# Keys and queries of three chunks as 2x2 block products, seven in place of eight, in a gated linear-attention and Mish kernel

## The chip, the cores and the metric

The kernel runs on one core of a Trainium2 chip. The metric is the device time of one execution, in microseconds (us), lower is better. Engines: PE (matrix products, with its weight load PEld), DVE (VectorE), ACT (ScalarE), POOL (GpSimd), SP (SyncE, which here only issues transfers). SBUF and PSUM are the on-chip memories; PE writes only PSUM, in banks of 128x512 fp32. A DMA moves data between DRAM and SBUF.

## The reference

x is 2048 rows of 512. Two branches read it and a gate mixes them:

```python
qkv = x @ wqkv                       # 512 -> q, k, v, 32 heads of 16
pq, pk = q @ w_phi, k @ w_phi        # per head, 16 x 16
phi = concat(softmax(p), softmax(-p))          # 32 features per head, of pq and of pk
kv = sum over rows of phi_k^T v ;  z = sum over rows of phi_k
o  = (phi_q kv) / (phi_q z + 1e-6) ; a = o @ wo
b  = mish(x @ w1 + b1) @ w2          # 512 -> 1376 -> 512
out = g * a + (1 - g) * b ,  g = sigmoid(sum(x * gate_w))
```

All is fp32. A product is made of three fp32r products: with each operand split as high + low part, high*high + high*low + low*high.

## The kernel before, in words

w_phi is first folded into the key and query weights on PE ("fuse"), so that one product of x gives pk or pq. Then come two stages.

Stage A goes over eight chunks of 256 rows (two tiles of 128, t = 0 and 1). Per chunk and tile PE makes three products, k (pk), v and q (pq), of 12 matmuls each: four slices of 128 of the 512 inputs times three of high/low. That is 72 matmuls for a chunk. After every second chunk the matmuls `kvp` add phi_k^T v of the last two chunks, 128 small ones. DVE turns each pk tile into features in nine steps, named in the order text as follows: `mx`, `mn` (maximum and minimum per head), `d0`, `d1` (p - max and min - p, into tile E of 128x1024), then after ACT's exponential (`E`) `S` (sums per head), `rS` (reciprocal), `ml` (E times the reciprocal). `z` adds E to zacc on POOL (L318): both operands 128x1024 in SBUF. ACT copies v and q out of PSUM (`ve`, `qe`); q goes to DRAM (pqd) for stage B. The next chunk's x is split by ACT (`xh`) and POOL (`xl`, L248). Two pieces of 128x1024 of w1 and w2 are split for stage B in every chunk: `wh` on ACT, `wl` on POOL (L370).

Stage B goes over four blocks of 512 rows: up projection, Mish, down projection, and the attention output of the same rows.

Order is written by hand. Texts such as EVEN, ODD, NEXT, LAST name the steps; `run` carries them out left to right, and every instruction is pinned to its place in its engine's queue. A step with `'` is of the previous chunk, one with `+` of the next. An engine runs its queue strictly in that order; between engines semaphores make an instruction wait for what it reads and for the buffer it overwrites. The E tiles have four buffers, PSUM tag "a" three banks and "dn" four, the x tiles ("tx") two.

```python
def proj(x, t, wh, wl, tag):
    for a, w in ((xh, wh), (xh, wl), (xl, wh)):
        for k in range(KT):
            mm(ps, a[k // 2][:, k % 2, sl], w[:, k, :], ...)
at(key, f"z{t}", lambda d=d: pin(G_.tensor_add(zacc, zacc, d["E"])))
run((EVEN, ODD)[c % 2] if c < NCH - 2 else NEXT if c < NCH - 1 else LAST, ("A", c), ("A", c - 1), ("B", 0))
```

All matmuls are recorded under the helper `mm` (L101), all ACT operations under `act` (L121), so the profile is read by tile names.

Of the kernel before, what the change touches and what calls it, by code (L numbers as in the profile page):

```python
# [15 lines left out]
P = 128  # L16
# [17 lines left out]
WARM = 6  # L34

# [16 lines left out]
    lq0+ k0 xh mx0 mn0 d00 d10 xl ldx k1 wh0 E0 wl0 ldw0 mx1 mn1 d01 d11 wh1 E1 S0 rS0 ml0 z0 v0 ve0 wl1 ldw1
# [37 lines left out]
def tile_gated_mix(ctx: ExitStack, tc: tile.TileContext, xT, wv, wkT, wqT, bd, w1a, w1b, b1, w2a, w2b, wo, out):  # L90
# [159 lines left out]
    def feat_ops(key, t, src, d):  # L250
# [7 lines left out]
        def dd(a):  # L258
# [3 lines left out]
            if a == 0:  # L262
# [16 lines left out]
    def scale_by(d, eng):  # L279
        pin(eng.tensor_mul(hv(d["E"][:, :]), hv(d["E"][:, :]), d["S"][:, :, None].to_broadcast([P, 2 * H, DH])))  # L280

    def a_ops(c):
        key = ("A", c)
        P_ = psA[c] = {}
        for t in range(2):
# [19 lines left out]

            def st(t=t):
# [11 lines left out]
            at(key, f"z{t}", lambda d=d: pin(G_.tensor_add(zacc, zacc, d["E"])))  # L318
# [14 lines left out]
        at(key, "kv", kv)  # L333
        if c + 1 < NCH:
# [6 lines left out]
            for j in range(2):  # L341
                at(key, "xl", lambda j=j: x_lo(c + 1, j, G_))
# [431 lines left out]
```

## Time and profile before

| | |
|---|---|
| runs | 456.2, 456.25 and 458.14 us, median 456.25 |
| span of the profiled execution, first to last instruction | 455.6 us; 0.65 us less than the median run |
| mean granted TensorE clock | 0.998 |
| PE busy | 445.6 us, 98% of the span |
| DVE, ACT, POOL busy | 306.8, 195.0 and 161.4 us |
| chunk 0's products start / chunk 1's / chunk 2's | 10.67 / 30.28 / 48.62 us |
| first matmuls of stage B's first block | 153.34 us |

A row of the timeline reads: start, duration (us), engine, line, operation, output <- inputs, shapes, how often, and in brackets the idle time before it with what ended it. An instruction's duration includes its start-up and its end, which overlap the neighbours', so instructions that follow each other closely start closer together than they last. A group by line gives the total and the mean in ns.

### The profile page before, as it was taken

Reading aid. Unit: us, or ns where it says so; the run is one execution under the profiler, and the core shown is the slowest. Engines: PE = TensorE matmul, PEld = TensorE weight load, DVE = VectorE, ACT = ScalarE, POOL = GpSimd, SP = SyncE. Lnnn points to the kernel's source line nnn. Section 1 sums busy time; section 2 is a strip of 40 time slices with the busy share of each in tenths; the row PEclk is TensorE's granted clock in tenths of the full one; section 3 lists DMA queues with packets and bytes.
Section 4 is the critical chain, followed back from the end, with each engine's and each line's share of the span. In section 5 each row is a group of like instructions: output and inputs, shape, how many; then the busy total and the mean of one; then the engine's idle time right before and its main releaser. Section 6 shows DMA issues by size and latency. Waiting matters only on the chain.

```text
span 455.6 us, 6980 instructions
## 1 busy us (share of the span) xinstructions
PE 445.6 (98%) x2772; PEld 363.4 (80%) x2772; DVE 306.8 (67%) x402; ACT 195.0 (43%) x265; POOL 161.4 (35%) x102
## 2 busy tenths in 40 slices
PE   7999999999999899999899999999999999999996
PEld 6888888888888678878687887887887888787885
DVE  2599459369399999799987985666967629611002
ACT  3554443443334645726337354434254553234220
POOL 3338777767862355221123212023212122221211
PEclk9999999999999999999999999999999999999999
DMA  7721513505523110313434050332041402030002
GB/s 284 247 83 56 168 53 129 186 8 179 183 82 106 47 23 2 94 46 86 146 94 138 17 158 14 108 115 54 23 119 53 112 19 94 1 81 13 1 1 92
DMA packets 25593, 40.07 MB, mean 88 GB/s; under 512 B 5716, under 2 KB 13908, under 8 KB 25560
## 3 DMA queue, kind: packets, MB, share of 16 engines
q1 hardware_dynamic: 25384, 39.35, 28.4%
q8 instruction: 22, 0.36, 0.3%
q10 hardware_dynamic: 144, 0.26, 0.2%
q14 instruction: 11, 0.09, 0.1%
q0 software_dynamic: 32, 0.01, 0.0%
HBM read 22.82 MB, written 8.40 MB: 69 GB/s over the span
## 4 chain that ended last, share of the span: by engine, by line
PE 61%; DVE 4%; ACT 1%; issue 0%
PE up L101 25%; PE down L101 24%; PE wo L101 10%; PE num L101 2%; DVE xbl L403 1%; DVE Sm L269 1%; DVE T L548 0%; DVE Dn L552 0%; DVE io L633 0%; ACT L121 0%; DVE tt L566 0%; DVE E L280 0%; DVE Dn L572 0%; ACT E L121 0%; DVE Sm L277 0%; ACT io L121 0%
## 5 line engine op out<-in xcount | busy, mean ns | idle before, releaser
L498 POOL TENSOR_TENSOR l<-act,h 128x512 fp32r<-128x512 f32 x44 | 60.7, 1380 | 224.2 <-ACT h L121 189.4
L121 ACT ACTIVATE act<-up,b1s 128x512 f32<-128x512 f32 x44 | 30.3, 689 | 91.5 <-PE up L101 90.3
L318 POOL TENSOR_TENSOR zacc<-zacc,E 128x1024 f32<-128x1024 f32 x16 | 39.7, 2482 | 45.8 <-DVE E L280 31.4
L121 ACT ACTIVATE E<-E 128x1024 f32<-128x1024 f32 x32 | 33.6, 1059 | 49.4 <-DVE E L265 49.4
L280 DVE TENSOR_TENSOR E<-E,Sm 128x1024 f32<-128x1024 f32 x32 | 44.0, 1375 | 1.1
L101 PE MATMUL wo<-woh,ohl 128*128 128x512 f32 x128 | 40.8, 390 | 1.2 <-DVE ohl L607 1.2
L269 DVE TENSOR_REDUCE Sm<-E 128x64 f32<-128x1024 f32 x32 | 38.7, 1209 | 3.8 <-ACT E L121 3.8
L101 PE MATMUL down<-w2ah,h 128*128 128x512 f32 x96 | 37.5, 390 | 0.0
L101 PE MATMUL down<-w2al,h 128*128 128x512 f32 x96 | 37.4, 389 | 0.0
L101 PE MATMUL down<-w2ah,l 128*128 128x512 f32 x96 | 37.4, 389 | 0.0
L633 DVE SCALAR_TENSOR_TENSOR io<-down,og_sb,io 128x512 f32<-128x512 f32 x16 | 11.3, 751 | 31.1 <-PE down L101 31.0
L256 DVE TENSOR_REDUCE mx<-proj 128x32 f32<-128x512 f32 x16 | 11.0, 689 | 30.8 <-PE proj L101 30.8
L101 PE MATMUL down<-w2bh,h 128*128 128x512 f32 x80 | 31.2, 391 | 0.0
L101 PE MATMUL down<-w2bl,h 128*128 128x512 f32 x80 | 31.1, 389 | 0.0
L101 PE MATMUL down<-w2bh,l 128*128 128x512 f32 x80 | 31.1, 389 | 0.0
L101 PEld LDWEIGHTS wo<-woh,ohl 128*128 128x128 f32 x128 | 24.0, 188 | 6.6 <-DVE ohl L607 1.6
L121 ACT ACT_TABLE_LOAD x19 | 24.4, 1283 | 10.1 <-PE up L101 9.8
L121 ACT ACTIVATE h<-act 128x512 fp32r<-128x512 f32 x44 | 27.8, 632 | 1.4
L607 DVE TENSOR_TENSOR ohl<-num,ohl 128x512 fp32r<-128x512 f32 x16 | 10.2, 678 | 26.4 <-ACT ohl L121 26.4
L101 PE MATMUL up<-xbl,w1ah 128*128 128x512 f32 x96 | 25.8, 391 | 1.5 <-DVE xbl L403 1.5
L101 PE MATMUL up<-xbh,w1ah 128*128 128x512 f32 x96 | 26.3, 396 | 0.2 <-ACT zb L121 0.2
L101 PE MATMUL up<-xbh,w1al 128*128 128x512 f32 x96 | 25.7, 389 | 0.0
(113 smaller groups left out, 970.6 us busy)
## 6 DMA issues: line engine op xcount, KB each, us to landing
xraw<-in_xT_dram SPq DMA_DIRECT2D x16, 512.0 KB, 4.8
eT<-tt SPq DMA_DIRECT2D x128, 64.0 KB, 2.0
pqd<-qs SPq DMA_DIRECT2D x16, 256.0 KB, 3.5
pq<-pqd SPq DMA_DIRECT2D x16, 256.0 KB, 2.8
out_dram<-io SPq DMA_DIRECT2D x16, 256.0 KB, 2.1
raw<-in_w1a_dram SPq DMA_DIRECT2D x3, 512.0 KB, 3.6
raw<-in_w2a_dram SPq DMA_DIRECT2D x3, 512.0 KB, 3.7
wT<-in_wkT_dram SPq DMA_DIRECT2D x4, 256.0 KB, 5.4
```

Of the source, the lines that this page charges most:

```text
L101: return pin(nc.tensor.matmul(*a, **k))
L121: return pin(A_.activation(out_, in_, fn, **k))
L256: pin(V.tensor_reduce(d[name], hv(src()), axis=AX.X, op=op))
L269: pin(V.tensor_reduce(d["S"], hv(d["E"][:, :]), axis=AX.X, op=ALU.add))
L280: pin(eng.tensor_mul(hv(d["E"][:, :]), hv(d["E"][:, :]), d["S"][:, :, None].to_broadcast([P, 2 * H, DH])))
L318: at(key, f"z{t}", lambda d=d: pin(G_.tensor_add(zacc, zacc, d["E"])))
L403: pin(V.tensor_sub(xb[b][1][:, :, sl], kt(raw[h], SC), f32(xb[b][0][:, :, sl])))
L498: pin(G_.tensor_sub(U[i]["l"], U[i]["a"], f32(U[i]["h"])))
L607: pin(V.tensor_sub(ohl[h, gp][:, 512:], num[h, gp], f32(ohl[h, gp][:, :512])))
L633: pin(V.scalar_tensor_tensor(io[t], dn[t], og_sb[:, i : i + 1], io[t], op0=ALU.mult, op1=ALU.add))
```

## The change

**Products.** In chunks 2, 3 and 4 (FAST) keys and queries are one product: x of the chunk as 2x2 blocks (row tile by half of the inputs) times the weights as 2x2 blocks (half of the inputs by key/query). Seven block products of six matmuls, named s1 to s7, take the place of eight. They need sums of weight blocks, t1 to t4, made once; sums of x's blocks, SX, made for each such chunk; and sums of products. `bc` (ACT) copies s1's bank into a second bank, `m7` (ACT) copies s7 to SBUF, `ca` (DVE) writes the second key bank from the two, `qa` (DVE) makes the second query tile. The weight sums need unsplit weights: ACT writes them from PSUM (`raw_k`, `wr0` to `wr3`), POOL makes t1, t3 and t4 (two operations) in chunk 0, DVE makes t2 in chunk 1, and ACT (`h0` to `h3`), POOL (`l0`, `l3`) and DVE (`l1`, `l2`) split them in chunk 1. The x sums are four POOL adds (`sa`), split by `sh` on ACT and `sl` on POOL, a chunk ahead.

**Feature sums.** In chunks 0 to 5 `z` is a DMA issued by POOL that writes or adds E to one of two DRAM tiles zd; in chunk 6 zd[0] is loaded by SP (`zld`) and zd[1] added to it by a DMA (`za`). Chunks 6 and 7 add on POOL as before. The memset of zacc goes.

**x's low parts** are made by DVE (`xl`) from the second chunk's on.

**Weights of stage B.** The pieces are loaded and split later: two in each of chunks 2, 3, 4 and three in each of 5 and 6. `kvp` of chunks 2 and 3 moves behind s7 of chunk 4 (`kk`). `fuse` now sets the start and stop flags once a bank.

The diff, cut to its core:

```diff
+FAST = range(2, 5)
 FIRST = """
-    S0 rS0 ml0 z0 ldw0 ldw1 S1 rS1 ml1 z1 q0 qe0 st0 q1 qe1 st1
+    S0 rS0 ml0 S1 rS1 ml1 z0 z1 q0 qe0 st0 q1 qe1 st1
...
+SECOND = """
+    k0 xh xl sa mx0 mn0 d00 d10 t2# ldx k1 E0 h1# l1# L0# L1# mx1 mn1 d01 d11 h0# l0# v0 E1 h2# l2# S0 rS0 ml0 h3# l3# sh0 sl0 ve0
+    v1 S1 rS1 ml1 z0 ve1 q0 qe0 st0 q1 sh1 sl1 z1 qe1 st1 kv' kv
+STRASSEN = """
+    s1 bc s7 m7 kk s2 xh xl mx0 mn0 s6 ca d00 d10 sa E0 ldx v0 ve0 sh0 sl0 more S0 rS0 s4 mx1 mn1 s5 qa st1 d01 d11 E1 ml0 z0
+    v1 S1 rS1 s3 ve1 qe0 st0 ml1 sh1 sl1 z1
...
+        at("W", "t1", lambda: pin(G_.tensor_sub(t1, k0, q0)))
+        at("W", "t3", lambda: pin(G_.tensor_sub(t3, q1, q0)))
+        at("W", "t4", lambda: pin(G_.tensor_sub(t4, q1, k1)))
+        at("W", "t4", lambda: pin(G_.tensor_add(t4, t4, t1)))
+        at("W", "t2", lambda: pin(V.scalar_tensor_tensor(t2, t1, -1.0, q1, op0=ALU.mult, op1=ALU.subtract)))
+        for i, r in enumerate((t1, t3, t2, t4)):
+            at("W", f"h{i}", lambda i=i, r=r: act(hl[0][i], r))
+            at("W", f"l{i}", lambda i=i, r=r: pin((V if i in (1, 2) else G_).tensor_sub(hl[1][i], r, f32(hl[0][i]))))
...
+            for o, a, b in ((s1, a21, a22), (s3, a11, a21), (s2, a11, s1), (s4, a12, s2)):
+                pin(G_.tensor_add(o, a, b))
...
+        def term(name, a, w, start, stop):
+            for ai, wi in ((0, 0), (0, 1), (1, 0)):
+                for k in range(2):
+                    mm(P_[name], a()[ai][:, k, :], w[wi][:, k, :], ...)
...
+            pin(V.tensor_add(P_["k", 1], P_["q", 0], P_["m7s"]))
+                pin(V.scalar_tensor_tensor(P_["qs", t], P_["q", 0], -1.0, P_["m7s"], op0=ALU.mult, op1=ALU.subtract))
...
-            at(key, f"z{t}", lambda d=d: pin(G_.tensor_add(zacc, zacc, d["E"])))
+                if c >= NCH - 2:
+                    pin(G_.tensor_add(Z["acc"], Z["acc"], d["E"]))
+                elif c:
+                    pin(G_.dma_start(zd[t][:, :], d["E"], accum_op=ALU.add))
+                else:
+                    pin(G_.dma_start(zd[t][:, :], d["E"]))
...
-                at(key, "xl", lambda j=j: x_lo(c + 1, j, G_))
+                at(key, "xl", lambda j=j: x_lo(c + 1, j, V if c else G_))
```

Three places show how the queues move. In the names a number ends each buffer: `wkr`, `wqr` hold the weight sums t1/t4 and t3/t2, `th`/`sh` and `tl`/`sl` high and low parts.

POOL, from the low parts of chunk 1's x to the start of chunk 1's work, before:

```order
L248 TENSOR_TENSOR xl_290<-xraw_86,xh_288 128x512
L248 TENSOR_TENSOR xl_291<-xraw_86,xh_289 128x512
L318 TENSOR_TENSOR zacc_124<-zacc_124,E_283 128x1024
L318 TENSOR_TENSOR zacc_124<-zacc_124,E_305 128x1024
L248 TENSOR_TENSOR xl_385<-xraw_296,xh_383 128x512
L248 TENSOR_TENSOR xl_386<-xraw_296,xh_384 128x512
```

and now:

```order
L253 TENSOR_TENSOR xl_304<-xraw_86,xh_302 128x512
L253 TENSOR_TENSOR xl_305<-xraw_86,xh_303 128x512
L299 TENSOR_TENSOR wkr_126<-wkr_126,wqr_127 128x1024
L300 TENSOR_TENSOR wqr_127<-wqr_127 128x1024
L301 TENSOR_TENSOR wkr_126<-wqr_127,wkr_126 128x1024
L302 TENSOR_TENSOR wkr_126<-wkr_126 128x1024
L430 DMA zd_124<-E_297 128x1024
L430 DMA zd_125<-E_319 128x1024
L323 TENSOR_TENSOR sraw_405<-xraw_310 128x256 x2
L323 TENSOR_TENSOR sraw_405<-xraw_310,sraw_405 128x256 x2
```

Four operations of 128x1024 stand where two did, then two DMA issues, and x's low parts of chunk 2 have left the queue.

DVE, from chunk 0's last feature step into chunk 1, before:

```order
L280 TENSOR_TENSOR E_305<-E_305,Sm_333 128x1024
L256 TENSOR_REDUCE mx_389<-proj_370 128x32
L256 TENSOR_REDUCE mn_391<-proj_370 128x32
L263 TENSOR_TENSOR E_393<-proj_370,mx_389 128x512
L265 TENSOR_TENSOR E_393<-mn_391,proj_370 128x512
L256 TENSOR_REDUCE mx_420<-proj_400 128x32
```

and now:

```order
L285 TENSOR_TENSOR E_319<-E_319,Sm_346 128x1024
L253 TENSOR_TENSOR xl_399<-xraw_310,xh_397 128x512
L253 TENSOR_TENSOR xl_400<-xraw_310,xh_398 128x512
L261 TENSOR_REDUCE mx_410<-proj_384 128x32
L261 TENSOR_REDUCE mn_412<-proj_384 128x32
L268 TENSOR_TENSOR E_414<-proj_384,mx_410 128x512
L270 TENSOR_TENSOR E_414<-mn_412,proj_384 128x512
L303 SCALAR_TENSOR_TENSOR wqr_127<-wkr_126,wqr_127 128x1024
L306 TENSOR_TENSOR tl_129<-wqr_127,th_128 128x1024
L261 TENSOR_REDUCE mx_440<-proj_420 128x32
```

Two operations stand ahead of the first feature step and two more between the tiles; a fifth, `tl` of t2, follows tile 1's d1 and stands ahead of S0. On ACT the part `th` for the first `tl` stands behind E of tile 0, that for the second behind E of tile 1.

PE, where chunk 4 begins, now (before, chunk 4 began with its twelve k0 matmuls, and these `kvp` stood ahead of it):

```order
L106 MATMUL proj_878<-th_128,sh_130 128x512 x2
L106 MATMUL proj_878<-tl_129,sh_130 128x512 x2
L106 MATMUL proj_878<-th_128,sl_131 128x512 x2
L106 MATMUL kvp_530<-E_639,v_663 32x64 x16
L106 MATMUL kvp_530<-E_699,v_727 32x64 x16
L106 MATMUL kvp_530<-E_780,v_804 32x64 x16
L106 MATMUL kvp_530<-E_840,v_868 32x64 x16
L106 MATMUL proj_877<-wkh_118,xh_761 128x512 x2
```

s7 ends, the four tiles' kvp follow, and s2 comes behind them.

More of the change, by code (lines that the diff above doesn't have):

```diff
@@ L209, in tile_gated_mix @@
     kvs = []
-    zacc = k4("zacc", "z")
-    pin(G_.memset(zacc, 0.0))
+    Z = {}
+    zd = [tc.dram_tile([P, 2 * D], F32, name=f"zd{t}") for t in range(2)]
     def fuse(staged, k):
@@ L677, in tile_gated_mix @@
     fsplit(wkh, wkl, 2)
+    raw_k(0)
+    raw_k(1)
     k_part(0)
```

174 lines of the change are left out of this document (133 added, 41 removed).

## The prediction

> **What bounds the kernel now.** I read the page first, its engine totals, then PE's waits, then the timeline of each engine through stage A.
>
> ```profile
> PE 445.6 (98%) x2772; PEld 363.4 (80%) x2772; DVE 306.8 (67%) x402; ACT 195.0 (43%) x265; POOL 161.4 (35%) x102
> PE fuse L101 <- DMA bds<-in_bd_dram: 2.1, 1, 2.1
> PE up L101 <- DVE xbl L403: 1.5, 1, 1.5
> PE wo L101 <- DVE ohl L607: 1.2, 1, 1.2
> ```
>
> PE is busy for 98% of the span, and the longest of its waits (total, times, longest, us) sum to 5 us. Nothing in stage A stops it. A matmul taken out is therefore time won, as long as PE then finds its operands ready; a new wait of PE is time lost, one for one.
>
> ```profile
> 30.28 1.07 PE L101 MATMUL proj<-wkh,xh 128*128 128x512 f32 x4
> 31.19 1.07 PE L101 MATMUL proj<-wkl,xh 128*128 128x512 f32 x4
> 32.10 1.07 PE L101 MATMUL proj<-wkh,xl 128*128 128x512 f32 x4
> ...
> 46.69 1.99 PE L101 MATMUL kvp<-E,v 128*32 128x64 f32 x128
> 48.62 1.20 PE L101 MATMUL proj<-wkh,xh 128*128 128x512 f32 x4
> ```
>
> Four matmuls advance PE by 0.91 us (30.28 to 31.19), so one costs 0.227, a tile's twelve 2.72 and a block product's six 1.36. Chunk 1 begins at 30.28; its kvp, at 46.69, needs the features of chunks 0 and 1; chunk 2 begins at 48.62.
>
> ```profile
> 28.07 1.23 DVE L280 TENSOR_TENSOR E<-E,Sm 128x1024 f32<-128x1024 f32 x1
> 29.22 1.21 DVE L269 TENSOR_REDUCE Sm<-E 128x64 f32<-128x1024 f32 x1
> 30.46 0.55 DVE L277 RECIPROCAL Sm<-Sm 128x64 f32<-128x64 f32 x1
> 31.05 1.90 DVE L280 TENSOR_TENSOR E<-E,Sm 128x1024 f32<-128x1024 f32 x1
> 33.20 0.69 DVE L256 TENSOR_REDUCE mx<-proj 128x32 f32<-128x512 f32 x1 [0.25 <-PE proj L101]
> 33.81 0.68 DVE L256 TENSOR_REDUCE mn<-proj 128x32 f32<-128x512 f32 x1
> 43.21 1.91 DVE L280 TENSOR_TENSOR E<-E,Sm 128x1024 f32<-128x1024 f32 x1
> 51.67 0.69 DVE L256 TENSOR_REDUCE mx<-proj 128x32 f32<-128x512 f32 x1 [6.55 <-PE proj L101]
> ```
>
> From start to start, DVE's steps on a 128x512 tile cost 0.60, S 1.25, rS 0.59, ml 1.15. Chunk 1's last ml ends at 45.1, 2.5 us before the half of kvp that needs it (46.69 + 0.97 = 47.66). That margin is what the change lives on.
>
> **DVE and POOL exclude each other.** This rule decides the sum, so here it is in a stretch late in stage A.
>
> ```profile
> 134.17 2.94 POOL L318 TENSOR_TENSOR zacc<-zacc,E 128x1024 f32<-128x1024 f32 x1
> 134.18 0.68 DVE L263 TENSOR_TENSOR E<-pq,mx 128x512 f32<-128x512 f32 x1
> 134.77 2.89 DVE L265 TENSOR_TENSOR E<-mn,pq 128x512 f32<-128x512 f32 x1
> 137.59 0.68 DVE L256 TENSOR_REDUCE mx<-proj 128x32 f32<-128x512 f32 x1
> 29.47 2.40 POOL L318 TENSOR_TENSOR zacc<-zacc,E 128x1024 f32<-128x1024 f32 x1 [5.84 <-DVE E L280]
> ```
>
> The two DVE subtractions read two SBUF tiles each. The first runs its 0.6 us, POOL's add waits that long (2.94 against 2.40), and the second, queued right behind the first, waits for the whole POOL instruction (2.89 against 0.68). So a DVE operation with two SBUF inputs and a POOL operation never overlap, and two queues with work alternate. Operations that read PSUM, such as mx above, are not held.
>
> **The change, part by part.**
>
> *Matmuls.* Three chunks times six matmuls go: 18 x 0.227 = **-4.1 us**.
>
> *Chunk 1, where the weight sums are finished.* PE's work there is unchanged; DVE's and POOL's is not. Rows of ACT and POOL:
>
> ```profile
> 13.22 0.60 ACT L121 ACTIVATE wkh<-fuse 128x512 fp32r<-128x512 f32 x1 [1.68 <-PE fuse L101]
> ...
> 18.44 2.07 ACT L121 ACTIVATE wqh<-fuse 128x512 fp32r<-128x512 f32 x4 [2.72 <-PE fuse L101]
> 20.36 1.17 ACT L121 ACTIVATE xh<-xraw 128x512 fp32r<-128x512 f32 x2
> 21.09 2.54 POOL L248 TENSOR_TENSOR xl<-xraw,xh 128x512 fp32r<-128x512 f32 x2 [2.83 <-ACT xh L121]
> 30.98 1.14 ACT L121 ACTIVATE xh<-xraw 128x512 fp32r<-128x512 f32 x2
> 35.72 1.06 ACT L121 ACTIVATE E<-E 128x1024 f32<-128x1024 f32 x1 [2.65 <-DVE E L265]
> 36.68 1.04 ACT L121 ACTIVATE w1ah<-raw 128x1024 fp32r<-128x1024 f32 x1
> ```
>
> Four more PSUM copies on ACT (0.5 each) move chunk 1's xh, and with it POOL's xl, about 2.1 us later: xl ends at 25.7. Chunk 1's first product needs it at 32.1, so this is hidden. POOL's t1 then runs to 28.05, where DVE's ml of chunk 0 is due (28.07), and the two alternate at 2.35 for POOL and 1.15 for DVE: ml0 to 29.2, t3 to 31.6, S and rS beside it to 31.0, ml1 31.6 to 32.75, t4's first operation to 35.1, the first xl to 35.7, t4's second operation to 38.05, the second xl to 38.65. Tile 0's mx, due at 33.20 before, starts at 38.65.
> From there: four steps to 41.05; t2, one operation of 128x1024, like ml 1.15, behind one of POOL's quarter-size adds (at most 0.65), to 42.6. ACT's exponential (0.96) and h1 (1.04) take from 41.05 to 43.1, so l1 runs 43.1 to 44.4 with a little waiting. Tile 1's four steps end at 46.8. Then h2 stands behind tile 1's exponential on ACT, 2.05 us, with DVE idle; l2 runs 48.85 to 50.0; S and rS to 51.85; ml0 waits for POOL's l3, taken when l2 let go (to 52.4), and ends at 53.55; S and rS to 55.4; ml1 ends at 56.6. kvp's last quarter (0.5) follows; behind it in PE's queue stands all of chunk 2, which starts at 57.1 instead of 48.6: **+8.5 us**.
> Bounds: with no mutual waits at all, ml1 of chunk 0 ends at 32.2, the two xl at 33.4, and the same chain (2.4; t2 and l1 to 39.0; 2.4; 2.05; l2; 1.85 and 1.15 twice) ends at 50.6, so chunk 2 starts at 51.1: +2.5. If t2, l1, l2 and ml1 each meet one POOL operation more (0.65 to 2.35), about 4.5 is added: +13. I take the laid-out value, since the alternation is in the rows.
>
> [...]
>
> *Chunks 2 to 4.* PE's chunk without waits is 66 x 0.227 = 14.97 (kk aside). DVE's is: two xl 1.2, eight feature steps 4.8, `ca` and `qa`, S and rS 3.7, ml 2.3, and an idle 1.0 for tile 0's exponential, since S0 stands right behind d1.
>
> ```profile
> L633 DVE SCALAR_TENSOR_TENSOR io<-down,og_sb,io 128x512 f32<-128x512 f32 x16 | 11.3, 751 | 31.1 <-PE down L101 31.0
> L248 POOL TENSOR_TENSOR xl<-xraw,xh 128x512 fp32r<-128x512 f32 x14 | 17.8, 1292 | 2.8 <-ACT xh L121 2.8
> L182 POOL DMA_DIRECT2D b1s<-in_b_dram x1 | 0.7, 676 | 0.0
> ```
>
> With 0.75 for `qa` (like io) and 0.65 for `ca` that is 14.4: as long as PE's chunk, before any wait for POOL. POOL has per chunk four quarter-size adds (0.65), two sl (1.29) and two weight pieces (2.40), 10 us, and two DMA issues (0.7 each, the nearest row). Laid out for chunk 2, counted from its start: xl after xh at 4.1 to 5.6, mx and mn to 6.8, ca to 7.45 (s4 wants it at 8.16), d0 and d1 to 8.65, exponential to 9.75, S and rS to 11.6, mx and mn to 12.8, qa to 13.5 (s3 wants it at 13.6, **+0.3** with handover), d0 and d1 to 14.65, ml0 behind a weight piece to 18.05, S and rS to 19.85, ml1 behind an sl to 21.4. That is 2.3 us behind where the next xl should start. In chunk 3 ca ends at 9.45 instead of 8.16 (1.3), qa is late by another 0.5, s2 waits 0.1 for ACT's bc: **+1.9**. In chunk 4 kk's last quarter, 4.2 after the start, needs chunk 3's ml1, due at 6.3: **+2.1**; the rest of the chunk catches up. Bounds: 0 (14.4 fits into 14.97 if no wait for POOL occurs); and, if in every chunk both ml wait for a whole weight piece (2.35) and both xl for a quarter-size add, 20.4 against 14.97, 16 in all less the 1.9 that kk takes of PE anyway: +14. I take the laid-out 4.3, since only one ml per chunk has a weight piece beside it.
>
> *What costs nothing.* The twelve zacc adds leave POOL (2.40 each) for DMA issues; E is rewritten two chunks, 30 us, later, and a transfer of 512 KB lands in 4.8 to 7.6 us, which leaves room for one that adds. The next DMA into the same zd waits on POOL for one issued a chunk earlier. In chunk 6 `zld` holds SP's queue and `za` holds POOL's until the DMAs of chunk 5 have landed; behind them stand weight pieces that stage B needs later and zacc, which ACT reads at 155.85.
>
> ```profile
> xraw<-in_xT_dram SPq DMA_DIRECT2D x16, 512.0 KB, 4.8
> ...
> raw<-in_wv_dram SPq DMA_DIRECT2D x2, 512.0 KB, 7.6
> ```
>
> The two rows give KB and the median us to landing.
>
> ```profile
> 121.24 0.69 DVE L256 TENSOR_REDUCE mx<-proj 128x32 f32<-128x512 f32 x1 [6.64 <-PE proj L101]
> 155.85 1.06 ACT L121 ACTIVATE zs<-zacc 128x1024 fp32r<-128x1024 f32 x1 [2.37 <-POOL zacc L318]
> ```
>
> In chunks 5 and 6 DVE's two xl stand where DVE waits for PE (6.64 us ahead of chunk 6), so stage B's start finds the same chain as before, with the same 1.5 us wait for xbl. The raw copies of the key weights (four of 0.6) lie in ACT's idle time ahead of 13.22 (1.68) and of 18.44 (2.72). The loads of weight pieces come later on SP, but the last piece is split in chunk 6, as before.
>
> **Sum.** -4.1 + 8.5 + 0.3 + 1.9 + 2.1 = +8.7 on a span of 455.6. The median run is 0.65 above the profiled span; added to 456.25 this gives 465.0 us.
>
> **Rivals.**
> *A, faster.* Everything added is hidden and 4.1 us come off: 452.2. For it speaks that PE never waits in stage A today. It needs all new waits together under 1.8 us, which means that chunk 1's chain ends by 49.9, 0.7 us below even my lower bound: the exponentials and the parts h1, h2 would have to cost DVE less than the 2 us each that ACT's rows give.
>
> ```profile
> 30.30:48.60 18.30, 18.30 (x201) 15.15 (x199) 14.12 (x17) 9.09 (x14) 15.79 (x8) 1.00 0.24 75
> ```
>
> This row is chunk 1: length, then busy time of PE, PEld, DVE, ACT, POOL.
>
> *B, no change.* DVE and POOL hardly meet: +2.5 in chunk 1, 0 to 2 in the fast chunks: 454.7 to 457. It speaks against it that POOL was busy for 15.8 of chunk 1's 18.3 us before, and DVE brings it five more operations to meet.
> *C, DVE sets the pace of the fast chunks.* Each of them takes 17 or more and kk's relief is used up; chunk 5's kvp waits too: 470 to 478.
>
> **How the numbers follow.** Chances: the forecast (a stall at chunk 1's kvp of 6 to 11, 1 to 8 after it; 459 to 469.5) 0.68, A 0.09, B 0.11, C 0.12. The likeliest is 465. 457 to 471 leaves out A, half of B and the far part of C, nearly 2 in 10. A measurement can tell 0.5%, 2.3 us, from no change. Faster is A and a sliver of B, 0.10; same is B, 0.10; slower is the rest, 0.80.
>
> **What would show it.** PE's waits should name kvp <- DVE E (about 8.5 us, near 47.7) as the longest; the timeline of DVE near 35 to 39 should show two xl of 2.5 to 3 us each between POOL's 128x1024 operations; chunk 4's kvp should wait about 2 for DVE's E; `proj` of s4 or s3 should wait 1 to 2 in chunk 3 for DVE. If the xl rows are 0.7 long, or h1 and h2 run ahead of the exponentials, the chunk 1 term fails; if PE waits for POOL (sl, or a zd DMA), a term is missing.

## The result and the profile after

On one chip the changed kernel took 468.34 us (median of 4 runs, 466.95 to 470.34), the kernel before 456.93 (4 runs, 456.2 to 458.14): a ratio of 1.0251, 95% interval 1.0212 to 1.029. The profiled execution has a span of 465.5 us (467.24 with what lies around it) against 455.6. So the medians differ by 11.4 us and the two profiles by 9.9: the profiled run is one of the two quicker of the four, and what follows accounts for the 9.9.

The engine totals, the granted clock in forty slices, and PE's two longest waits (total, times, longest) of the changed kernel:

```profile
PE 444.5 (95%) x2754; PEld 361.5 (78%) x2754; DVE 326.2 (70%) x423; ACT 205.8 (44%) x286; POOL 159.4 (34%) x114
PEclk9999699999999999999999999999999999999999
PE kvp L106 <- DVE E L285: 9.1, 2, 5.8
PE proj L106 <- DVE proj L367: 2.0, 1, 2.0
```

PE is busy for 95% of the span where it was 98%. The 18 matmuls are gone (2754 for 2772), and two waits have come that the kernel before did not have: 9.1 us at `kvp`, in two pieces, and 2.0 us at `proj`. Where they lie, from the timeline of PE:

```profile
46.06 1.10 PE L106 MATMUL kvp<-E,v 128*32 128x64 f32 x64
52.97 1.08 PE L106 MATMUL kvp<-E,v 128*32 128x64 f32 x32 [5.81 <-DVE E L285]
57.35 1.08 PE L106 MATMUL kvp<-E,v 128*32 128x64 f32 x32 [3.29 <-DVE E L285]
58.36 1.22 PE L106 MATMUL proj<-wkh,xh 128*128 128x512 f32 x2
...
84.71 0.74 PE L106 MATMUL proj<-sh,xh 128*128 128x512 f32 x2 [1.99 <-DVE proj L367]
...
94.86 2.11 PE L106 MATMUL kvp<-E,v 128*32 128x64 f32 x128
```

Chunk 1's `kvp` waits once for each of the chunk's two `ml`; chunk 2 then starts at 58.36 instead of 48.62. Chunk 3's s4 waits for `ca`. Chunk 4's four tiles of `kvp` wait for nothing. Two stretches of this timeline (length; busy time and count of PE, PEld, DVE, ACT, POOL; granted clock; DMA share; GB/s):

```profile
29.65:58.36 28.71, 19.61 (x202) 16.02 (x200) 24.68 (x23) 10.53 (x15) 21.28 (x16) 0.86 0.44 139
58.36:60.77 2.41, 2.41 (x10) 1.95 (x7) 0.00 (x0) 0.00 (x0) 2.33 (x5) 0.58 0.85 107
```

The second is s1 behind the wait: its six matmuls (the count of ten takes in neighbours at the edges) take 2.41 us at a granted clock of 0.58, where six take 1.36 at full clock; s7's pairs of 0.62 us follow. From the starts of the chunks' first products, the span divides so (us; "predicted" is the prediction's sum):

| stretch | before | after | difference | predicted |
|---|---|---|---|---|
| up to chunk 1 | 30.28 | 29.65 | -0.6 | 0 |
| chunk 1, with kvp before and after | 18.34 | 28.71 | +10.4 | +8.5 |
| chunk 2 | 16.45 | 16.03 | -0.4 | -1.4 + 0.3 |
| chunk 3; before with kvp (1.93) | 18.34 | 17.66 | -0.7 | -1.4 - 1.9 + 1.9 |
| chunk 4; after with kvp | 16.45 | 17.24 | +0.8 | -1.4 + 1.9 + 2.1 |
| the rest | 355.7 | 356.2 | +0.5 | 0 |
| span | 455.6 | 465.5 | +9.9 | +8.7 |

What made `kvp` wait is on DVE and POOL:

```profile
34.13 4.02 DVE L253 TENSOR_TENSOR xl<-xraw,xh 128x512 fp32r<-128x512 f32 x2
38.08 0.68 DVE L261 TENSOR_REDUCE mx<-proj 128x32 f32<-128x512 f32 x1
42.62 1.23 DVE L306 TENSOR_TENSOR tl<-wqr,th 128x1024 fp32r<-128x1024 f32 x1 [0.59 <-ACT th L126]
48.31 1.22 DVE L306 TENSOR_TENSOR tl<-wqr,th 128x1024 fp32r<-128x1024 f32 x1 [2.07 <-ACT th L126]
54.58 2.62 DVE L285 TENSOR_TENSOR E<-E,Sm 128x1024 f32<-128x1024 f32 x1
...
78.46 4.38 DVE L253 TENSOR_TENSOR xl<-xraw,xh 128x512 fp32r<-128x512 f32 x2 [0.29 <-ACT xh L126]
```

```profile
29.74 3.38 POOL L301 TENSOR_TENSOR wkr<-wqr,wkr 128x1024 f32<-128x1024 f32 x1
33.21 3.26 POOL L302 TENSOR_TENSOR wkr<-wkr 128x1024 f32<-128x1024 f32 x1
54.53 1.58 POOL L329 TENSOR_TENSOR sl<-sraw,sh 128x512 fp32r<-128x512 f32 x1
...
79.89 1.71 POOL L323 TENSOR_TENSOR sraw<-xraw 128x256 f32<-128x256 f32 x2
81.28 2.15 POOL L323 TENSOR_TENSOR sraw<-xraw,sraw 128x256 f32<-128x256 f32 x2
```

The two xl take 4.02 us beside t4's operation, which itself takes 3.26 in place of 2.40: the alternation. The first of the pair lasts 2.88 us, the second 1.22. Chunk 1 began 0.63 us earlier here than in the kernel before, from which the prediction counts, so its rows are best compared from the chunk's start: tile 0's mx starts 8.43 us in (predicted 8.37), the first `tl` 12.97 (12.82), the second 18.66 behind 2.07 us of idle DVE (18.57 behind 2.05). Only the last row is off: the last ml ends 27.55 us in (26.32). It met a low part of the x sums on POOL (54.53) and took 2.62 us where 1.15 was laid out. In chunk 3 the same pair of xl takes 4.38 us, beside the quarter-size adds.

### The profile page after: what moved, and what is told of

Same layout as the page of the kernel before. It is cut to its first block, busy times and chain, and to the rows that moved or that the text cites. A ratio compares the mean times of both kernels' runs of the same rounds, so it can differ in the third digit from the quotient of the medians.

```text
span 465.5 us, 7015 instructions
## 1 busy us (share of the span) xinstructions
PE 444.5 (95%) x2754; PEld 361.5 (78%) x2754; DVE 326.2 (70%) x423; ACT 205.8 (44%) x286; POOL 159.4 (34%) x114
## 4 chain that ended last, share of the span: by engine, by line
PE 80%; DVE 15%; ACT 2%; issue 1%; DMA 1%; DVEq 0%; ACTq 0%
PE up L106 25%; PE down L106 24%; PE proj L106 18%; PE wo L106 9%; DVE E L285 2%; DVE Sm L274 2%; PE num L106 2%; PE fuse L106 1%; DVE E L268 1%; PE kvp L106 1%; DVE mx L261 1%; DMA wT<-in_wkT_dram 1%; DVE xbl L532 1%; DVE Sm L282 1%; DVE E L270 1%
## 5 line engine op out<-in xcount | busy, mean ns | idle before, releaser
L532 DVE TENSOR_TENSOR xbl<-xraw,xbh 128x1024 fp32r<-128x1024 f32 x8 | 12.2, 1562 | 19.8 <-ACT xbh L126 19.8
L106 PE MATMUL wo<-wol,ohl 128*128 128x512 f32 x64 | 24.9, 389 | 0.0
```

Of the source, the lines that this page charges most:

```text
L106: return pin(nc.tensor.matmul(*a, **k))
L532: pin(V.tensor_sub(xb[b][1][:, :, sl], kt(raw[h], SC), f32(xb[b][0][:, :, sl])))
```

## The experiments

The theory: the loss is the supply of the block products, DVE's chain in chunk 1 above all, made longer by its meetings with POOL; the rest of the change costs nothing. The kernel before stood beside each of them, at 457.0 to 457.8 us. Ratios are to it.

### e1_no_pool_sums: POOL's weight sums left out

```diff
-        at("W", "t1", lambda: pin(G_.tensor_sub(t1, k0, q0)))
-        at("W", "t3", lambda: pin(G_.tensor_sub(t3, q1, q0)))
-        at("W", "t4", lambda: pin(G_.tensor_sub(t4, q1, k1)))
-        at("W", "t4", lambda: pin(G_.tensor_add(t4, t4, t1)))
```

Chunks 2 to 4 so multiply with raw weight blocks in place of t1, t3 and t4 and compute something else; the instructions are the same but for these four.

> The changed kernel without GpSimd's four operations of 128x1024 that make the weight sums t1, t3 and t4 (the raw key and query weights are used in their place, so three chunks compute something else; every other instruction stays). Theory (DVE and POOL exclude each other, and DVE's two xl of chunk 1 stood between these four operations): the two xl take 0.7 us each, tile 0's mx starts at about 34 instead of 38.1, PE's wait at chunk 1's kvp falls from 9.1 to 4 to 5 us, and the whole is 4 to 6 us below the changed kernel, 462 to 464. Rival (the wait comes from ACT's order alone, the parts h1 and h2 behind the exponentials): the wait stays above 8 us and the time within 1 us of the changed kernel.

Measured: 465.68 us, ratio 1.0174 (1.0135 to 1.0212). DVE and PE in its timeline:

```profile
33.50 1.28 DVE L253 TENSOR_TENSOR xl<-xraw,xh 128x512 fp32r<-128x512 f32 x2
51.25 2.62 DVE L285 TENSOR_TENSOR E<-E,Sm 128x1024 f32<-128x1024 f32 x1
...
49.65 0.65 PE L106 MATMUL kvp<-E,v 128*32 128x64 f32 x32 [1.51 <-DVE E L285]
54.02 1.08 PE L106 MATMUL kvp<-E,v 128*32 128x64 f32 x32 [3.72 <-DVE E L285]
```

Without the four operations the xl pair takes 1.28 us instead of 4.02 and the wait is 5.2 instead of 9.1: 3.9 us of it were meetings with the weight sums. Chunk 1 is 4.3 us shorter (24.42), but the time only 2.7, which misses the expected 462 to 464. The chunks 2 and 3 became 0.7 and 1.3 longer: the matmuls behind their waits ran longer (in chunk 2, from 55.04 on, pairs of 1.00 to 1.22 us for the usual 0.62 over 3.6 us, where the changed kernel has 2.4 us of slow pairs; in chunk 3, from 82.11 on, pairs of 0.82 to 1.06 us over 4.0 us), and the profiled run began 1.0 later. What is left, 5.2 us, is the length of DVE's chain and the meetings with the later parts: the last ml takes 2.62 us here too.

### e2_parts_early: the high parts ahead of the exponentials

```diff
-    k0 xh xl sa mx0 mn0 d00 d10 t2# ldx k1 E0 h1# l1# L0# L1# mx1 mn1 d01 d11 h0# l0# v0 E1 h2# l2# S0 rS0 ml0 h3# ...
+    k0 xh xl sa h1# h0# mx0 mn0 d00 d10 t2# ldx k1 E0 h2# l1# L0# L1# mx1 mn1 d01 d11 l0# v0 E1 l2# S0 rS0 ml0 h3# ...
```

> Only the order of ACT and of t2's split changes: h1 and h0 stand ahead of tile 0's exponential, h2 ahead of tile 1's. Rival (ACT's order holds DVE up): DVE's idle 0.59 and 2.07 us ahead of the two tl in chunk 1 go and PE's wait falls by 2.7 us, from 9.1 to 6.4. Theory (mutual exclusion counts more): with h0 early, GpSimd's tl of t1 is ready when DVE's t2 ends and runs first, so DVE's first tl waits for it (about 2 us); the wait of PE falls by 0 to 1 us only.

Measured: 470.73 us, ratio 1.0289 (1.0242 to 1.0336); waits at `kvp` 11.9 us, 9.6 of them in chunk 1. DVE's two `tl` and tile 0's ml:

```profile
42.52 3.43 DVE L306 TENSOR_TENSOR tl<-wqr,th 128x1024 fp32r<-128x1024 f32 x1
48.27 1.21 DVE L306 TENSOR_TENSOR tl<-wqr,th 128x1024 fp32r<-128x1024 f32 x1
51.23 2.65 DVE L285 TENSOR_TENSOR E<-E,Sm 128x1024 f32<-128x1024 f32 x1
```

DVE's idle time ahead of both, 2.7 us, is gone, and the second `tl` starts only 0.6 us earlier in its chunk (18.03 us in for 18.66): the first, ready sooner, met a POOL operation, as the theory said, and took 3.43 in place of 1.23. Then tile 0's ml met another and took 2.65 in place of 1.54, and the wait is not 0 to 1 us shorter, as the theory had it, but 0.5 longer. The gap for ACT was not what set the length; taking it away handed the time to the alternation. The other 2.3 us are a wait at chunk 4's `kvp`, after an ml that took 3.48 us.

### e3_xl_pool: x's low parts back on POOL

```diff
-                at(key, "xl", lambda j=j: x_lo(c + 1, j, V if c else G_))
+                at(key, "xl", lambda j=j: x_lo(c + 1, j, G_))
```

> One part of the change is undone: x's low parts are made by GpSimd in all chunks. Theory: DVE's xl cost far more than their own 1.2 us a chunk, since each waits for a GpSimd operation; without them chunk 1's mx starts 4 us earlier, PE's wait at chunk 1's kvp falls by 3 to 5 us and the 2.0 us wait of chunk 3 for ca goes: 5 to 7 us below the changed kernel, 461 to 463. Rival (DVE is short of time only by the work itself): 1.2 us less in chunk 1, and GpSimd, with 2.6 us more, is late with sl: the time falls by under 2 us.

Measured: 464.6 us, ratio 1.0157 (1.0131 to 1.0183). PE, and DVE's t2:

```profile
51.20 1.08 PE L106 MATMUL kvp<-E,v 128*32 128x64 f32 x32 [3.71 <-DVE E L285]
55.56 1.08 PE L106 MATMUL kvp<-E,v 128*32 128x64 f32 x32 [3.28 <-DVE E L285]
...
36.81 1.21 DVE L303 SCALAR_TENSOR_TENSOR wqr<-wkr,wqr 128x1024 f32<-128x1024 f32 x1
```

The wait falls from 9.1 to 7.0, and chunk 3's wait for `ca` is gone: its 1.99 us came from the xl pair that took 4.38 there. So this part of the change costs 2.1 us in chunk 1 and 2.7 in chunk 3 (14.97 for 17.66); 1.2 of it is lost again in chunk 2, whose first two products ran longer (4.92 us for 3.79; the first five pairs took 1.03 to 1.22 us each for the usual 0.62). Both the wait and the time fell less than expected (3 to 5 us, and 461 to 463). Tile 0's mx did start 4.0 us earlier in its chunk, but the second `tl` then met POOL and took 3.04 us for 1.22: again the meeting moved.

The row of t2 shows 1.21 us for it, as long as a tensor_tensor of that size (`tl`, 1.22 at 48.31 in the changed kernel), so the prediction's estimate for it, that of ml, fits where nothing holds it up.

### e4_z_pool: feature sums back on POOL, no DMAs

```diff
-                if c >= NCH - 2:
-                    pin(G_.tensor_add(Z["acc"], Z["acc"], d["E"]))
-                elif c:
-                    pin(G_.dma_start(zd[t][:, :], d["E"], accum_op=ALU.add))
-                else:
-                    pin(G_.dma_start(zd[t][:, :], d["E"]))
+                pin(G_.tensor_add(Z["acc"], Z["acc"], d["E"]))
```

The memset of zacc at the start comes back with it, and chunk 6's `zld` and `za` go.

> Another part is undone: the feature sums are GpSimd's adds in all chunks, with no DMA to DRAM. Theory: twelve operations of 2.4 us come back to the queue that DVE waits for; PE's wait at chunk 1's kvp grows by 1 to 4 us and the fast chunks by up to 1 us each: 468 to 474. Rival (the adding DMAs slow other transfers, or lengthen what lies outside the span, which was 1.7 us in the changed kernel's runs): the span gets longer by under 1 us or shorter, and the time outside it falls back to about 0.7.

Measured: 474.19 us, ratio 1.0378 (1.0341 to 1.0414); `kvp` waits 12.2 us, 10.9 of them in chunk 1.

```profile
34.34 5.68 DVE L253 TENSOR_TENSOR xl<-xraw,xh 128x512 fp32r<-128x512 f32 x2
```

The xl pair now meets still more of POOL's queue (5.68 for 4.02). The DMAs are worth 5.9 us in this kernel: they take out POOL operations that DVE would have met. What lies around the span stayed (1.9 us, 1.7 with the DMAs), so the DMAs are not what lies there.

### e6_plain_products: no block products, everything else kept

```diff
-FAST = range(2, 5)
+FAST = range(0)
...
+PLAIN = """
+    k0 xh xl mx0 mn0 d00 d10 ldx k1 E0 mx1 mn1 d01 d11 v0 E1 more S0 rS0 ml0 ve0 v1 S1 rS1 ml1 z0 ve1 q0 qe0 st0 q1 z1 qe1 st1
+"""
...
```

The weight sums, raw copies and x sums go with them; chunks 1 to 4 run PLAIN, with kvp behind every second.

> The rest of the change without the block products: twelve matmuls per tile everywhere, no weight sums and no x sums; the feature sums by DMA, xl on DVE and the later weight pieces stay. Theory: none of that is on PE's path by itself; within 1 us of the kernel before. Rival (the DMAs or xl on DVE cost by themselves): 2 us or more above it, with PE waiting in stage A.

Measured: 457.27 us, ratio 1.0006 (0.9995 to 1.0016). PE's three longest waits:

```profile
PE fuse L109 <- DMA bds<-in_bd_dram: 1.9, 1, 1.9
PE up L109 <- DVE xbl L535: 1.5, 1, 1.5
PE wo L109 <- DVE ohl L739: 1.2, 1, 1.2
```

None lies in stage A. DMA sums, xl on DVE and the later weight pieces change nothing measurable by themselves; the loss comes only with the block products and their supply, beside which xl on DVE does cost (e3).

### e5_filler: PE kept busy through the wait

```diff
             (kvp,) = kvs
+            if c == 1:
+                fill = psum("fill", "a")
+                for i in range(35):
+                    mm(fill, xs[1][0][0][:, 0, :P], wkh[:, i % KT, :], start=(i == 0), stop=(i == 34))
```

> The changed kernel with 35 matmuls more, whose result nothing reads, between the kvp of chunk 0 and that of chunk 1, that is, inside PE's wait. Theory (PE's clock is granted lower after the idle stretch): PE still waits about 1 us in that place, chunk 2's first matmuls run at the full 0.227 us a matmul (the changed kernel's s1 took 2.4 us instead of 1.36, at a granted clock of 0.58), and the time falls by about 1 us. Rival (s1 was slow for another reason, such as its operands): s1 takes 2.4 us again and the time stays.

Measured: 468.31 us, ratio 1.0244 (1.0226 to 1.0263). PE's timeline, and the stretch of s1 and s7 (columns as above):

```profile
47.77 8.23 PE L106 MATMUL fill<-wkh,xh 128*128 128x512 f32 x35
58.14 0.65 PE L106 MATMUL kvp<-E,v 128*32 128x64 f32 x32 [1.56 <-DVE E L285]
```

```profile
58.73:61.58 2.85, 2.85 (x19) 2.36 (x13) 0.00 (x0) 0.58 (x1) 2.77 (x5) 1.00 0.93 139
```

With PE busy the clock stays at 1.00: a quarter of `kvp` lasts 0.65 for 1.08, and s1 and s7 take 2.85 us where the changed kernel took 3.79 (58.36 to 62.15). So the slow s1 was the clock, not a late operand: the wait of 1.56 us that is left has full speed behind it. In this one profile chunks 1 and 2 are 1.25 us shorter together; the median did not move (468.31 for 468.34), and the profiled run began 0.7 us later and lost another 0.6 from chunk 6 on. The mechanism is shown, the microsecond in the median is not, and why stays open.

### f1 and f2: the supply in another order

Weight sums, chunk 1's x and the split of the x sums go earlier, h0 and h3 later, the part l2 and x's low parts up to chunk 5's move from DVE to POOL, and `kvp` of chunks 0 and 1 moves behind chunk 2's s7, as the change did it for chunk 4. So this is another division of the work too, not its order alone. The lines that go are left out here but for three.

```diff
 FIRST = """
+    xh xl fq v0 fh0 fh1 wr0 wr1 t1# fh2 fh3 wr2 wr3 t3# t4# fl0 fl1 mx0 mn0 d00 d10 fl2 fl3 ldx ve0 E0 mx1 mn1 d01 d11 v1 ve1 E1
 SECOND = """
+    k0 xh xl sa h1# sh0 sl0 mx0 mn0 d00 d10 t2# l1# ldx k1 L0# L1# E0 h2# l2# mx1 mn1 d01 d11 v0 E1 sh1 sl1 S0 rS0 ml0 h0# l0# ve0
+    v1 S1 rS1 ml1 z0 ve1 q0 qe0 st0 q1 h3# l3# z1 qe1 st1
...
-            at("W", f"l{i}", lambda i=i, r=r: pin((V if i in (1, 2) else G_).tensor_sub(hl[1][i], r, f32(hl[0][i]))))
+            at("W", f"l{i}", lambda i=i, r=r: pin((V if i == 1 else G_).tensor_sub(hl[1][i], r, f32(hl[0][i]))))
-        if odd in FAST:
+        if odd in FAST or odd == 1:
-                at(key, "xl", lambda j=j: x_lo(c + 1, j, V if c else G_))
+                at(key, "xl", lambda j=j: x_lo(c + 1, j, V if c >= 5 else G_))
```

f2 is the same with `V if c >= 2` and, in STRASSEN, xl behind d10.

> The three-chunk block products with the supply rearranged: chunk 1's xh and xl stand ahead of the query weights' split, so that GpSimd's weight sums end before DVE's two ml of chunk 0; h1 and the x sums' split go early, l1 follows t2, l2 goes to GpSimd, kvp of chunks 0 and 1 moves behind s7 of chunk 2, and GpSimd makes xl up to chunk 5's. Theory (the loss was mutual waits in chunk 1, nothing in the products): no wait of PE above 1 us at chunk 1's or 2's kvp, clock 1.00 at chunk 2's start, chunks 2 to 4 within 0.7 us of 14.97 (plus 1.93 where kvp stands), and the whole 2 to 4 us below the kernel before. Rival (seven block products need more of DVE, ACT and GpSimd than a chunk has room for): waits move into chunks 2 to 4, 2 us or more in each, and the time is not below the kernel before.

> As f1, but in chunks 2 to 6 DVE makes xl, and in the fast chunks it stands behind tile 0's d1, where DVE waits for the exponential, and no longer ahead of mx. Theory: the 2.0 us wait of chunk 3 for ca came only from xl's place ahead of mx; PE waits for ca nowhere, and the time is within 1 us of f1, 2 to 4 us below the kernel before. Rival: the two xl still meet GpSimd's operations and make DVE late with qa or ml: PE waits 1 to 3 us for DVE in chunks 3 or 4.

Measured: f1 457.24 us, ratio 1.0005 (0.9989 to 1.0021); f2 459.47, 1.0042 (1.0026 to 1.0058). DVE, POOL and PE in f1's timeline, then the stretch behind PE's row:

```profile
36.17 4.53 DVE L303 SCALAR_TENSOR_TENSOR wqr<-wkr,wqr 128x1024 f32<-128x1024 f32 x1
50.59 1.57 DVE L285 TENSOR_TENSOR E<-E,Sm 128x1024 f32<-128x1024 f32 x1
...
34.98 2.55 POOL L253 TENSOR_TENSOR xl<-xraw,xh 128x512 fp32r<-128x512 f32 x2
37.48 1.43 POOL L323 TENSOR_TENSOR sraw<-xraw 128x256 f32<-128x256 f32 x2
38.88 2.42 POOL L323 TENSOR_TENSOR sraw<-xraw,sraw 128x256 f32<-128x256 f32 x2
...
52.31 0.65 PE L106 MATMUL kvp<-E,v 128*32 128x64 f32 x32 [2.01 <-ACT xh L126]
```

```profile
52.89:57.33 4.44, 4.44 (x19) 3.51 (x13) 1.29 (x2) 0.00 (x0) 4.44 (x4) 0.62 0.93 150
```

11.1 of the 11.4 us are back, but not the 2 to 4 more that were expected. Chunks 1, 3 and 4 take 16.32, 14.96 and 17.11 us, within 0.2 of what their matmuls need; chunk 2 takes 20.93 where 16.9 would do. Its `kvp` waits 2.01 us. The row names ACT's xh, which had long been done; the ml that ends at 52.16 is what it needs. The 4.44 us behind it run at a clock of 0.62, which costs about as much again as the wait. The largest single delay ahead of that ml is t2, 4.53 us for 1.21. It stood ready from 36.17 while POOL ran the second xl and three of the four quarter-size adds, one behind the other; only the fourth waited for it.

In f2 the rival came true. Its xl pair took 2.11 us in chunk 3, the ml of the chunks 2 and 3 met POOL (3.33 and 2.66 us), and PE waits 0.34 us at s3 of chunk 3 and 1.58 at chunk 4's `kvp`: the two chunks take 2.4 us more than f1's.

### f3, f4, f5, f6: one wait at a time

f3 puts chunk 2's `kvp` behind s6; f4 moves h0 and h3 behind the copies bc and m7; f5 does in chunk 4 what f3 did in chunk 2, splits t4 ahead of t1, and puts chunk 1's second zd DMA behind both; f6 also puts chunk 0's two zd DMAs behind the x sums on POOL. Each holds the ones ahead of it. f6 against f1:

```diff
 FIRST = """
-    S0 rS0 ml0 S1 rS1 ml1 z0 z1 q0 qe0 st0 q1 qe1 st1
+    S0 rS0 ml0 S1 rS1 ml1 q0 qe0 st0 q1 qe1 st1
 SECOND = """
-    k0 xh xl sa h1# ... S0 rS0 ml0 h0# l0# ve0
-    v1 S1 rS1 ml1 z0 ve1 q0 qe0 st0 q1 h3# l3# z1 qe1 st1
+    k0 xh xl sa z0' z1' h1# ... S0 rS0 ml0 ve0
+    v1 S1 rS1 ml1 z0 ve1 q0 qe0 st0 q1 qe1 st1
...
+        text = STRASSEN
+        if c in (2, 4):
+            text = text.replace("m7 kk s2", "m7 s2").replace("s6 ca", "s6 kk ca")
+        if c == 2:
+            text = text.replace("m7 s2", "m7 h3# l3# h0# l0# z1' s2")
```

> As f1, with the block of kv matmuls of chunks 0 and 1 behind chunk 2's s6 in place of behind its s7. In f1 that block waits 2.01 us for VectorE's scaling, which ends at 52.16 us, and the eight or so microseconds behind the wait run at a lower clock, so that chunk 2 takes 20.93 us where its matmuls need about 16.9 (chunk 4 of f1, with a block of its own, takes 17.11). With the four products s1, s7, s2, s6 (1.36 us each in f1's undisturbed chunks) ahead of the block, its last quarter starts at about 45.9 + 5.45 + 1.5 = 52.9 us, behind 52.16: no wait, no lower clock. Theory (all the change's loss is the supply of the block products): chunk 2 takes 16.9 to 17.5, 3.4 to 4.0 us less than f1's: 453.2 to 453.9 us, ratio to before 0.991 to 0.994, no wait over 0.3 us in the chunks 1 to 4. Rival (the time comes back at a later wait, as the filler's gain did in e5): a new wait of 1 to 2 us at s4 or in chunk 3 (VectorE behind), 455 to 457 us.

> As f3, with the two ACT copies of weight sums that only chunk 2's s5 and s4 read (h0, h3, 1.05 us each, and GpSimd's two remainders behind them) moved from ahead of chunk 2's copies bc and m7 to behind them. In f3 s2 waits 1.89 us for bc, which ScalarE reaches at 50.7 us behind those two copies though s1 ended at about 47.9, and the matmuls behind the wait run at a lower clock: chunk 2 takes 20.9 us there. Theory: bc starts 2.1 us earlier, at about 48.6, s2 waits 0 to 0.3 us, the block of kv matmuls starts at about 52 and its last quarter at 53.5 finds VectorE's scaling done (52.7): chunk 2 takes 16.9 to 17.4, 3.5 us less: median 452 to 453.2, ratio to before 0.988 to 0.991. Rival (supply is short in sum, and each repair moves the wait): GpSimd's remainders are now late for s4 or for chunk 3 and 1 to 2 us of wait appear there, with the clock's loss behind them: 455 to 457, ratio 0.995 to 1.0.

> As f4, with chunk 4's block of kv matmuls behind s6 as well, the remainder that s4 reads ahead of the one that s5 reads, and the DMA that adds chunk 1's second feature tile behind both on GpSimd's queue (GpSimd stood idle 2.07 us at that DMA in f4). f4's losses by its trace: chunk 2 1.2 us, chunk 3 1.2 us (s2 waits 0.65 for a copy), chunk 4 3.6 us (the block waits 1.82 us, and the eight microseconds behind it run at a lower clock). Theory (each loss has a place, and supply suffices): the block of chunk 4 waits for nothing, chunks 2, 3 and 4 take 17.2, 15.2 to 16.0 and 17.2 us in place of 18.3, 16.2 and 20.7: 454 to 455 us, ratio to before 0.992 to 0.995. Rival (supply is short in sum, the wait moves on): chunk 4 keeps its 20 us or chunk 5 gets the wait, 457 to 460.

> As f5, with the two DMAs that write chunk 0's feature tiles behind GpSimd's sums of x for chunk 2 in place of ahead of its remainders of x: in f4 GpSimd waited 1.66 and 2.37 us at them for VectorE's scaling while the remainders and sums stood behind. Theory (supply is a matter of order): GpSimd's sums of x end 3 to 4 us earlier, ScalarE's first copy of them at about 36.5 us in place of 39.8, and whatever waits f5 still has in the chunks 2 and 3 shrink by 0.5 to 1.5 us in sum: 453 to 454.5 us, ratio 0.989 to 0.993, or 0 to 1.5 us below f5. Rival: GpSimd's earlier instructions collide with VectorE's scaling of chunk 0 and its first difference, these grow by 1 to 2 us each, and the block of kv matmuls in chunk 2 waits again: 1 to 3 us above f5.

| kernel | chunk 1 | 2 | 3 | 4 | sum | median | ratio |
|---|---|---|---|---|---|---|---|
| before | 18.34 | 16.45 | 18.34 | 16.45 | 69.6 | | |
| changed | 28.71 | 16.03 | 17.66 | 17.24 | 79.6 | 468.34 | 1.0251 |
| f1 | 16.32 | 20.93 | 14.96 | 17.11 | 69.3 | 457.24 | 1.0005 (0.9989 to 1.0021) |
| f3 | 16.33 | 20.89 | 14.97 | 17.1 | 69.3 | 456.03 | 0.9978 (0.996 to 0.9997) |
| f4 | 16.32 | 18.32 | 16.18 | 20.74 | 71.6 | 459.65 | 1.004 (1.0025 to 1.0056) |
| f5 | 16.32 | 18.38 | 16.09 | 17.31 | 68.1 | 455.68 | 0.9974 (0.9963 to 0.9985) |
| f6 | 16.32 | 17.11 | 15.80 | 17.46 | 66.7 | 454.86 | 0.9951 (0.9935 to 0.9968) |

(The chunks from one profile each; every row holds the same two blocks of `kvp`.) In f3 and f4 the rival was right that the wait moves on, though in f3 to another product than it named, and f4 came out beyond even its 455 to 457. f3's `kvp` waits for nothing, but s2 now waits for bc, and f4 repairs that and gets the wait back in chunk 4. PE in f3, then POOL and PE in f4 with the stretch behind PE's row:

```profile
51.35 1.03 PE L106 MATMUL proj<-wkh,xh 128*128 128x512 f32 x2 [1.89 <-ACT proj L126]
```

```profile
52.28 0.88 POOL L428 DMA_DIRECT2D zd<-E  x1 [2.07 <-DVE E L285]
...
86.86 0.65 PE L106 MATMUL kvp<-E,v 128*32 128x64 f32 x32 [1.82 <-DVE E L285]
```

```profile
86.86:91.87 5.01, 5.01 (x44) 3.98 (x45) 1.29 (x2) 0.00 (x0) 4.34 (x4) 0.66 1.00 251
```

Both waits, under 2 us, were followed by more than 4 us at about two thirds of the clock (f3: 0.62 from 51.35 to 55.89). The POOL row is the one f5 changes: POOL stood idle 2.07 us at a DMA with the remainders of t1 and t4 behind it. In f5 chunk 4 is as expected (17.31), while chunk 2 is not (18.38 for 17.2; its `kvp` still waits 0.74), and the time misses the expected 454 to 455 by 0.7. f6 lets POOL's x sums start 4.0 us earlier in chunk 1 (3.9 us into it for 7.9). Its only wait in the chunks 1 to 7, then chunks 2 to 4 (columns as above), then DVE's t2 and the last ml of chunk 1:

```profile
PE proj L106 <- ACT proj L126: 0.4, 1, 0.4
```

```profile
47.61:64.72 17.11, 17.11 (x196) 14.14 (x194) 14.00 (x17) 8.96 (x13) 13.70 (x12) 1.00 0.53 106
64.72:80.52 15.80, 15.42 (x68) 12.23 (x66) 13.30 (x16) 8.88 (x15) 15.72 (x14) 1.00 0.80 199
80.52:97.98 17.46, 17.41 (x196) 14.07 (x194) 16.11 (x18) 9.19 (x14) 14.50 (x9) 1.00 0.79 214
```

```profile
38.62 1.57 DVE L303 SCALAR_TENSOR_TENSOR wqr<-wkr,wqr 128x1024 f32<-128x1024 f32 x1
50.81 1.23 DVE L285 TENSOR_TENSOR E<-E,Sm 128x1024 f32<-128x1024 f32 x1
```

t2 takes 1.57 instead of 4.53, the last ml of chunk 1 ends at 52.0, ahead of the `kvp` quarter that needs it, and the clock is 1.00 in all three chunks. The four chunks take 66.7 us against 69.6: in this profile 2.9 of the 4.1 us of the 18 matmuls are won, in the medians 2.1 (454.86 to 457.0). f6 is 2.9% faster than the changed kernel (468.34) and faster than the kernel before by 0.5%, its whole interval on that side. That is 0.8 below f5, as expected, but above the 453 to 454.5 that were expected outright.

## Why the prediction was right, and where its steps failed

The call was slower, 465.0 us, 457 to 471; measured 468.34.

- *18 x 0.227 = -4.1.* Right, as far as seen: with no wait in the way (f1) a block-product chunk takes 14.96.
- *Chunk 1, +8.5.* The mechanism held: DVE's chain, made longer by POOL, is what `kvp` waits for. The +10.4 is 1.9 more than the sum had, in two places. The last ml met an x part on POOL that the layout left out and ended 1.2 us late; and the last quarter of `kvp`, behind the wait, took 1.0 us at a granted clock of 0.50 where the sum had 0.5 us. (The quarter between the two waits was slow too, 1.08 us at 0.50, which cost nothing, since PE had to wait again.) That mx starts within 0.1 us of the prediction is partly luck: POOL was 1.9 us further along in the chunk than laid out (t4's second operation starts 3.56 us in, laid out 5.42), tile 0's ml of chunk 0 waited for t3 and not t3 for it, and so only the first xl met a 128x1024 operation (2.88 and 1.22 us, where 2.5 to 3 each were named as the sign). e1 and e3 take 3.9 and 2.1 us out of the wait by removing the two partners of the meeting. The choice between bounds (the laid-out value over the +2.5 without meetings) is borne out; e2 shows that shortening the chain elsewhere only moves the meeting.
- *Chunk 2, +0.3 at s3.* Failed: no product waited. The chunk took 1.05 us more than its matmuls need for a reason that no step foresaw, s1 at a clock of 0.58 (e5 shows that it is the clock).
- *Chunk 3, +1.9.* A loss came at the place that was named (PE waits 1.99 us for `ca`; the chunk lost 2.7 in all, 17.66 against 14.97), but by luck, since the cause was another. The step had chunk 2's two ml behind POOL's weight piece and sl, ending 2.3 us late. The timeline of the changed kernel has it otherwise:

```profile
71.26 5.83 POOL L499 TENSOR_TENSOR w1al<-raw,w1ah 128x1024 fp32r<-128x1024 f32 x2
73.61 1.21 DVE L285 TENSOR_TENSOR E<-E,Sm 128x1024 f32<-128x1024 f32 x1
```

  The ml fell on the seam between two weight pieces, and it was POOL that waited. DVE was not behind: chunk 3's xl started 4.07 us into the chunk, as laid out for a chunk on time (4.1). `ca` was late because this xl pair met sl and the quarter-size adds and took 4.38 us, and e3, which moves xl away, has no such wait.
- *Chunk 4, +2.1 at kk.* Failed: the chunk lost 0.3. The step carried the lateness of chunk 3's step on; chunk 3's last ml ended 4.1 us into chunk 4 instead of 6.3. In f4, where an ml did wait for a weight piece (3.18 us at 80.20), this very wait appeared (1.82).
- *What costs nothing.* e6 confirms it: 1.0006.
- *Sum.* +8.7 against +9.9 on the span, nearer than its terms: chunk 1 was 1.9 too small, chunks 2 and 3 0.7 each, and chunk 4 was 1.8 too large. The alternation was also taken to be stricter than it is: in f1 POOL ran four operations while a DVE operation stood ready. That operations which read PSUM are not held is in the trace of the kernel before: mx took 0.69 us at 33.20, beside a POOL add (2.39 us at 33.12). The 0.65 for what lies around the span compared a median with another run's span; in runs that give both it is about 1.7 for either kernel (456.33 with a span of 454.6 before, from a later series; 467.24 with 465.5 after), so it cancels in the ratio.
- *The rivals.* B needed DVE and POOL hardly to meet; the rows of 4.02 and 3.26 us rule it out. C needed every fast chunk at 17 and more; they took 16.0, 17.7 and, with kvp, 17.2. A was not the change's fate, but f6 comes part of the way to it, which the prediction took to be out of reach because it asked what this order could do, not another.

## What to carry to other kernels

When work leaves the busiest engine, lay out the queues of the engines that feed it, in time, over the whole stretch before the operands are due: the matmuls saved here were worth 4.1 us, and two helpers' queues cost 9.1 at one place. Where two engines hold each other up, as DVE and POOL did here (a pair of xl took 4.02 us beside POOL's queue, 1.28 without its weight sums), moving one operation to the other engine or a little earlier may only choose another partner to wait for; f4 repaired one wait and came out slower than f3. A wait of PE of some two microseconds can cost nearly twice its length (f1: 2.01 us, and another 1.7 in the 4.44 us behind it, at a clock of 0.62), so price it with the granted clock of the matmuls behind it.

## What the runs showed of the hardware that was not expected

**The clock behind a wait.** Waits of 1.82 to 2.01 us were followed by 4 to 5 us at a mean granted clock of 0.62 to 0.66 in f1, f3 and f4; two block products took 4.4 to 4.5 us there instead of 2.7, another 1.7 to 1.8 us each. Waits of the same length were followed by full speed elsewhere: the changed kernel's 1.99 us at 84.71 has a pair of 0.74 us behind it and then the usual 0.62 (clock 1.00 from 84.71 to 87.60), and f2's 1.98 us likewise (0.72, 0.63; clock 1.00 from 52 to 58). The wait for `ca` in chunk 3 has both outcomes at one place: full speed in the changed kernel, pairs of 0.82 to 1.06 us over the next 4.0 us in e1 (a wait of 2.04 us, ended at 82.11). What decides it these runs don't tell.

**Neighbours in the queue.** Two DVE subtractions one behind the other took 1.28 us where POOL was idle (the kernel before, at 9.52), 4.02 and 4.38 (changed kernel) and 5.68 (e4) where it had a queue: in the changed kernel each of the two was held up (2.88 and 1.22 us, 1.42 and 3.04, where one of DVE's steps of that size takes 0.68). The turns need not alternate one by one: in f1 DVE's t2 waited through four POOL operations in a row, three of them of quarter size, and in the changed kernel's chunk 3 the second xl through three. What gives DVE its turn stays open.

**A DMA that adds.** Issuing a DMA that adds 512 KB from SBUF into DRAM held POOL for 0.88 us in the changed kernel (median of ten, the longest 1.20; the two that only write, 0.55 and 0.59), and the twelve zd transfers landed in 7.6 us (median); PE's and DVE's waits in that trace name none of them.
